# Broadcasting attention denominators through DRAM and transposing rows by DMA in a four-layer kernel on one core

## The chip, the core and the metric

The kernel runs on one core of a Trainium2 chip. The core has a matrix engine (TensorE; PE in the profile, its weight loads PEld), a vector engine (VectorE, DVE), an activation engine (ScalarE, ACT), GpSimd (POOL) and SyncE (SP), which here issues every DMA. Each engine takes its instructions in the order in which they were put on it and waits on semaphores. SBUF is the on-chip memory of 128 partitions; PSUM, in eight banks of 2 KB per partition, takes the results of matmuls.

The metric is the device time of one execution in microseconds, as a median of several runs.

## The reference

A sequence of 2048 rows of 576 numbers goes through four residual layers: linear attention (A), MLP (B), and once more A and B with the same weights.

```python
# A: x = x + attention(layernorm(x)); 32 heads of 18
qkv = layernorm(x) @ wqkv
phi = lambda t: jnp.where(t > 0, t + 1, jnp.exp(t)) + 1e-6
pq, pk = phi(q), phi(k)
kv  = einsum("bhsd,bhse->bhde", pk, v);  z = einsum("bhsd->bhd", pk)
o   = einsum("bhqd,bhde->bhqe", pq, kv) / (einsum("bhqd,bhd->bhq", pq, z) + 1e-6)
x   = x + o @ wo
# B: a second layernorm, then 576 -> 4608 -> 576
x   = x + gelu(layernorm(layernorm(x)) @ w1 + b1) @ w2 + b2
```

B's input is normalised twice in a row; the kernel folds the two into one by its constants. Matmul operands are bfloat16, sums are float32. Everything of A after the projections needs the sum `kv` over all 2048 rows, so an attention layer has two halves.

## The kernel before, in words

The 2048 rows are 16 row tiles of 128. The residual stream x lies in DRAM (`x_d`, float32) between layers. Every layer begins with the normalised rows transposed: `yT` holds 5 blocks of 128 columns (576 padded to 640) by 2048 rows, in bfloat16.

**Normalisation.** `LNPipe` holds row tiles on their way and `tick` (L232) moves each one stage on: load from `x_d` (L242, only in layers 1 and 3, for rows whose sum is long past), statistics on DVE (L249 to L260), the power -0.5 on POOL (L265), the normalised row `y` (L280 on POOL or L284 on DVE) into a ring of four buffers, and last five TensorE transposes into one PSUM bank of its own, `tp` (L297), with a copy to `yT` by ACT (L299) or DVE (L301). The loops of the layers call `tick` at fixed places.

**Attention, first half.** For each row tile: `k_proj` (L370), `v_proj` (L382, L385), and `kv_acc` (L400), which adds to the sums kv and z in PSUM. The feature map phi takes two ACT passes and two DVE passes (`phi_from_psum`). `q_proj` (L406) makes phi(q) for one of 5 head groups (7 heads of 18 are 126 partitions; the last group has 4) and one chunk of 512 rows; of its 20 calls 13 lie in the first half.

**Attention, second half, called the tail.** `kv_wo` (L451) multiplies kv by wo once per head group; `kvwo` is copied out by ACT (L458) or DVE (L456). `den_stage` (L466 to L476) makes the denominators of a chunk of 512 rows, their reciprocals on DVE, and spreads them with a mask into `quad_rden`. `scale_stage` (L482 to L485) broadcasts them over the 18 numbers of each head by a matmul with the 0/1 matrix `head_bc`, copies the result out of PSUM by ACT and multiplies phi(q) by it on DVE. `wo_stage` (L493) then makes the output rows of one row tile with ten matmuls in one of two two-bank PSUM buffers, and `residual` (L349) adds the old row, which `prefetch_xo` loaded four row tiles earlier into a ring of five buffers (`x_ring`; L333 in layer 0, as bfloat16 from the input, L336 later), into one of three `xn` buffers; L355 stores it. The first four row tiles of the next layer are normalised here.

**MLP.** Four chunks of 512 rows. Nine groups `m1_group` (L593) make the 4608 hidden numbers, gelu on ACT (L589); then for each of the chunk's four row tiles 72 matmuls (L640) make the output row. `feed_next` puts the next chunk's rows into `LNPipe`: two in the fifth and seventh group, two in the first output row. `tick(transposes=0)` keeps transposes out of the groups. In layer 1 every finished row also goes to `LNPipe` for layer 2.

**Order.** A planner puts the instructions of each engine into a list, from the order in which the program writes them and its own estimate of when each is ready; so an instruction written later can stand ahead (the load at L242 stands ahead of the last store of L355 at the end of each tail). Semaphore waits follow from that. `pe` chains the TensorE instructions of the layers in the written order, `chained` the early DMAs; `add_manual_dep` with `NOSYNC` only orders. The weights are loaded in pieces in layer 0's first half (`late_pieces`), w2 (L195) last, and POOL builds masks there (`masks`).

PSUM before: three banks for `h` (all projections, denominators, broadcasts, hidden numbers), one for `tp`, four for the two accumulators.

Of the kernel before, what the change touches and what calls it, by code (L numbers as in the profile page):

```python
# [15 lines left out]
P = 128  # L16
# [15 lines left out]
C1 = 1.0 + 1e-6  # L32


def build(tc, A_x, A_wqkv, A_wo, B_w1, B_b1, B_w2, B_b2, out, dbg=None, n_layers=4):
    nc = tc.nc
    dbg = dbg or {}
    with ExitStack() as ctx:
        const = ctx.enter_context(tc.tile_pool(name="const", bufs=1))
        ps_h = ctx.enter_context(tc.tile_pool(name="ps_h", bufs=3, space=PSUM))  # L40
        ps_tp = ctx.enter_context(tc.tile_pool(name="ps_tp", bufs=1, space=PSUM))
# [18 lines left out]
        head_bc = const.tile([P, G, P], BF16, name="head_bc")  # L60
        quad_mask = const.tile([P, 4, P], BF16, name="quad_mask")
# [12 lines left out]
        def inner_diag(tile_, lead, n):  # L74
# [5 lines left out]
        hb = head_bc[:, :, 0:126].rearrange("p g (h d) -> p g h d", h=7)  # L80
# [6 lines left out]
        ] + inner_diag(head_sel, lambda sign: [[126 * sign, G]], H) + [  # L87
            fill(quad_mask, 1.0),
            select(quad_mask[:], 0.0, ALU.is_ge, 0, [[-32, 4], [0, P]], 1),
            select(quad_mask[:], 0.0, ALU.is_ge, 31, [[32, 4], [0, P]], -1),  # L90
            fill(head_bc, 0.0),
        ] + [select(hb, 1.0, ALU.not_equal, -32 * quad, [[-7, G], [-1, 7], [0, DH]], 1) for quad in range(4)]
# [20 lines left out]
        NX = 5  # L113
        x_ring = [const.tile([P, D], F32, name=f"x_ring{i}") for i in range(NX)]
        x_d = dpool.tile([NT, P, D], F32, name="x_d")

        work = ctx.enter_context(tc.tile_pool(name="work", bufs=2))
        blk = ctx.enter_context(tc.tile_pool(name="blk", bufs=NF))

# [89 lines left out]
        def bias_casts():  # L209
# [4 lines left out]
                      [(lambda i=i: piece_w2(i)) for i in range(6)] + [piece_b1_dma]  # L214

        state = dict(ycnt=0, vcnt=0, xl=0)
        pool_last = dict(norm=None)
        dve_last = dict(norm=None, sum=None, phi=None)

        class LNPipe:  # L220
# [3 lines left out]
            def feed(self, xt, t, kind, norm_eng, evac_eng="dve", load_from=None, after=None):  # L224
                self.items.append(dict(stage=(0 if load_from is None else -1), xt=xt, t=t, kind=kind,
                                       norm=norm_eng, evac=evac_eng, load=load_from,
                                       after=after))

            def busy(self):
                return len(self.items)  # L230

            def tick(self, transposes=1):  # L232
                for it in list(self.items):
                    st = it["stage"]
                    if st == 4:
                        if transposes == 0:
                            continue
                        transposes -= 1
                    if st == -1:
                        xn = x_ring[3 + state["xl"] % 2]  # L240
                        state["xl"] += 1
                        load = nc.sync.dma_start(out=xn[:], in_=x_d[it["load"]])  # L242
                        if it["after"] is not None:
                            tc.add_manual_dep(load.ins, it["after"], NOSYNC, reason="loads give way")
                        it["xt"] = xn
                    elif st == 0:
                        xt = it["xt"]
                        stt = work.tile([P, 2, 6], F32, name="ln_st", bufs=4)
                        first = nc.vector.bn_stats(out=stt[:, 0, :], in_=xt[:, 0:HALF])  # L249
                        second = nc.vector.bn_stats(out=stt[:, 1, :], in_=xt[:, HALF:D])  # L250
                        if it["after"] is not None:
                            for stats in (first, second):
                                tc.add_manual_dep(stats.ins, it["after"], NOSYNC, reason="statistics give way")
                        mv = work.tile([P, 2], F32, name="ln_mv", bufs=6)
                        nc.vector.bn_aggr(out=mv[:], in_=stt[:])
                        u = work.tile([P, 1], F32, name="ln_u", bufs=4)
                        if it["kind"] == "A":
                            nc.vector.tensor_scalar(out=u[:], in0=mv[:, 1:2], scalar1=EPS, scalar2=None, op0=ALU.add)  # L258
                        else:
                            nc.vector.tensor_scalar(out=u[:], in0=mv[:, 1:2], scalar1=1.0 + EPS, scalar2=EPS * EPS,  # L260
                                                    op0=ALU.mult, op1=ALU.add)
                        it["mv"], it["u"] = mv, u
                    elif st == 1:
                        rstd = work.tile([P, 1], F32, name="ln_rstd", bufs=6)
                        nc.gpsimd.tensor_tensor(out=rstd[:], in0=it["u"][:], in1=neg_half[:], op=ALU.pow)  # L265
                        it["rstd"] = rstd
                    elif st == 2 and it["norm"] != "dve":
# [4 lines left out]
                    elif st in (2, 3):  # L272
# [14 lines left out]
                        if it["kind"] == "B":  # L287
                            nc.gpsimd.tensor_copy(out=y[:, D:DPAD], in_=y[:, 4 * P:D])
# [3 lines left out]
                    elif st == 4:  # L292
# [3 lines left out]
                        for k in range(KD):  # L296
                            pe(nc.tensor.transpose(out=tp[:, k, :], in_=y[:, k * P:(k + 1) * P], identity=ident[:]))  # L297
# [458 lines left out]
```

## Time and profile before

| | us |
|---|---|
| median of 3 runs | 790.49 (790.04 to 790.71) |
| profiled execution, its span | 790.0 |
| TensorE busy | 778.6 |
| ACT busy | 341.2 |
| DVE busy | 264.5 |
| POOL busy | 125.7 |
| layer 0: first half, and tail | 0 to 71, 71 to 112 |
| layer 1 (MLP) | 112 to 401 |
| layer 2: first half, and tail | 401 to 459, 459 to 501 |
| layer 3 (MLP) | 501 to 790 |

The profile is one execution. It shows the busy time of each engine, the span in 40 slices (a digit is the busy share in tenths; DMA is the mean share of 16 DMA engines), groups of instructions by line and tile, who waited for whom, the chain of work that ended last (followed back from the last instruction) and the time line of each engine. A time line gives start, duration, engine, line, operation, output and inputs, shapes and count. Matmuls are pipelined and their busy times overlap, so that the distance between starts tells what one costs. The DMA issues are listed with their size and the time from issue to landing.

### The profile page before, as it was taken

The page shows a single profiled execution, that of the slowest core. Times are in us where ns is not written, and L with a number is a line of the kernel's source. Part 1 is how long each engine was busy: PE and PEld are TensorE (multiplying, and loading weights), DVE is VectorE, ACT ScalarE, POOL GpSimd, SP SyncE. Part 2 cuts the span into 40 slices and gives each one's busy share as a digit, 9 for nine tenths or more (in the row PEclk, how much of TensorE's full clock was granted, in tenths as well). Part 3 has the DMA queues.
Part 4 walks back from the last instruction along what each step waited for, and adds up shares of the span by engine and source line. Part 5 has one row for each costly group of instructions (what it writes and reads, how often), then busy time and mean ns, then how long its engine had stood idle before and what let it go on. Part 6 is the DMA issues. An engine that isn't in the chain of part 4 may idle for free.

```text
span 790.0 us, 16121 instructions
## 1 busy us (share of the span) xinstructions
PE 778.6 (99%) x6807; PEld 507.0 (64%) x6813; DVE 264.5 (33%) x711; ACT 341.2 (43%) x754; POOL 125.7 (16%) x211
## 2 busy tenths in 40 slices
PE   8999999999999999999999999999999999999998
PEld 5776654685478458646887766547745864685476
DVE  6786862135023504300344478433200300010000
ACT  5888646304610660164047785471066017304600
POOL 4571402013010301200100004211110110001000
PEclk9999999999999999999999999999999999999999
DMA  9990372012021202200210007611210110011000
GB/s 274 259 285 24 129 260 71 1 62 90 1 61 46 76 2 75 76 1 1 80 42 1 2 16 240 240 47 53 61 39 3 60 61 1 9 46 38 2 23 23
DMA packets 43506, 56.92 MB, mean 72 GB/s; under 512 B 10283, under 2 KB 28075, under 8 KB 43435
## 3 DMA queue, kind: packets, MB, share of 16 engines
q1 hardware_dynamic: 43434, 55.91, 23.1%
q8 instruction: 53, 0.87, 0.5%
q14 instruction: 19, 0.15, 0.1%
HBM read 39.38 MB, written 16.52 MB: 71 GB/s over the span
## 4 chain that ended last, share of the span: by engine, by line
PE 92%; DVE 4%; DMA 2%; ACT 1%; issue 1%; POOL 0%; DVEq 0%; POOLq 0%; ACTq 0%
PE m_ps L640 36%; PE h_ps L593 20%; PE hp_ps L593 16%; PE q_ps L406 5%; PE k_ps L370 5%; PE v_ps L385 3%; PE tp L297 2%; PE v_ps L382 2%; PE wo_ps L493 2%; DMA x_d<-xn 2%; DVE xn L349 1%; PE kvacc L400 1%; PE warm_ps L171 1%; DVE pq L485 1%; DVE rden L474 0%
## 5 line engine op out<-in xcount | busy, mean ns | idle before, releaser
L640 PE MATMUL m_ps<-w_sb,hT 128*128 128x288 bf16 x2304 | 289.9, 286 | 0.0
L640 PEld LDWEIGHTS <-hT 128*128 128x128 bf16 x2304 | 223.2, 98 | 57.9 <-issue 3.4
L593 PEld LDWEIGHTS <-w_sb 64*128 64x128 bf16 x2304 | 124.5, 94 | 136.5 <-issue 1.9
L593 PE MATMUL hp_ps<-yT,w_sb 64*128 64x512 bf16 x1152 | 178.0, 376 | 0.0
L593 PE MATMUL h_ps<-yT,w_sb 64*128 64x512 bf16 x1152 | 148.0, 376 | 0.0
L598 ACT COPY relay_sb<-relay_sb 128x1 f32<-128x1 f32 x144 | 28.5, 198 | 276.3 <-PE h_ps L593 234.2
L589 ACT ACTIVATE hT<-h_ps,b1T 128x512 bf16<-128x512 f32 x144 | 91.0, 683 | 44.5 <-PE h_ps L593 44.5
L301 DVE COPY yT<-tp 128x640 bf16<-128x640 bf16 x40 | 19.6, 490 | 239.5 <-PE tp L297 239.5
L265 POOL TENSOR_TENSOR ln_rstd<-ln_u,neg_half 128x1 f32<-128x1 f32 x64 | 36.0, 562 | 357.5 <-DVE ln_u L258 193.5
L589 ACT ACTIVATE hT<-hp_ps,b1T 128x512 bf16<-128x512 f32 x144 | 91.1, 692 | 0.0
L339 POOL TENSOR_TENSOR x_ring<-x_ring,b_bc 128x576 f32<-128x576 f32 x32 | 40.8, 1279 | 159.5 <-DMA x_ring<-x_d 159.5
L593 PE MATMUL h_ps<-yT,w_tail 64*128 64x512 bf16 x144 | 54.1, 376 | 0.0
L593 PE MATMUL hp_ps<-yT,w_tail 64*128 64x512 bf16 x144 | 54.1, 376 | 0.0
L349 DVE TENSOR_TENSOR xbf<-m_ps,x_ring 128x576 bf16<-128x576 f32 x16 | 12.0, 752 | 117.6 <-PE m_ps L640 117.6
L406 PE MATMUL q_ps<-yT,wqkv_sb 128*126 128x512 bf16 (+1 forms) x200 | 50.0, 382 | 0.5 <-ACT phi_a L321 0.5
L493 PE MATMUL wo_ps<-kvwo,pq 126*128 126x288 bf16 (+1 forms) x320 | 43.8, 285 | 3.5 <-DVE xn L349 3.0
L370 PE MATMUL k_ps<-wqkv_sb,yT 128*128 128x288 bf16 x320 | 44.3, 286 | 0.0
L319 ACT ACTIVATE phi_e<-k_ps 128x288 bf16<-128x288 f32 x64 | 27.0, 422 | 35.9 <-PE k_ps L370 35.8
L493 PEld LDWEIGHTS <-pq 126*128 126x128 bf16 (+1 forms) x320 | 30.6, 97 | 14.8 <-issue 5.0
L322 DVE TENSOR_SCALAR phi_e<-phi_e 128x288 bf16<-128x288 bf16 (+2 forms) x104 | 30.7, 295 | 27.3 <-ACT phi_e L319 26.9
L593 PEld LDWEIGHTS <-w_tail 64*128 64x128 bf16 x288 | 27.1, 94 | 17.1
L370 PEld LDWEIGHTS <-yT 128*128 128x128 bf16 x320 | 30.9, 98 | 11.1
(90 smaller groups left out, 643.6 us busy)
## 6 DMA issues: line engine op xcount, KB each, us to landing
x_ring<-x_d SPq DMA_DIRECT2D x72, 288.0 KB, 3.0
x_d<-xn SPq DMA_DIRECT2D x48, 288.0 KB, 2.2
w_sb<-in_B_w_dram SPq DMA_DIRECT2D x6, 864.0 KB, 10.4
w_sb<-in_B_w_dram SPq DMA_DIRECT2D x9, 512.0 KB, 5.3
x<-in_A_x_dram SPq DMA_DIRECT2D x16, 144.0 KB, 4.1
x_ring<-in_A_x_dram SPq DMA_DIRECT2D x16, 144.0 KB, 3.2
out_dram<-xbf SPq DMA_DIRECT2D x16, 144.0 KB, 1.8
wqkv_sb<-in_A_wqkv_dram SPq DMA_DIRECT2D x3, 576.0 KB, 5.8
```

What stands on the lines that cost most here:

```text
L265: nc.gpsimd.tensor_tensor(out=rstd[:], in0=it["u"][:], in1=neg_half[:], op=ALU.pow)
L319: act_last["exp"] = nc.scalar.activation(out=e[0:rows, 0:n], in_=ps_ap, func=ACT.Exp).ins.name
L322: nc.vector.tensor_scalar(out=e[0:rows, 0:n], in0=e[0:rows, 0:n], scalar1=1.0, scalar2=1e-6, op0=ALU.min, op1=ALU.add)
L339: nc.gpsimd.tensor_tensor(out=xo, in0=xo, in1=b2_bc[:], op=ALU.add)
L370: pe(nc.tensor.matmul(kp[:, 0:HALF], lhsT=yT[:, k, tok], rhs=wqkv_sb[:, k, D + half * HALF: D + (half + 1) * HALF], start=(k == 0), stop=( ...
L385: pe(nc.tensor.matmul(vp[:, 1, 0:324], lhsT=yT[:, k, tok], rhs=wqkv_sb[:, k, 2 * D + 252: 3 * D], start=(k == 0), stop=(k == KD - 1)))
L406: pe(nc.tensor.matmul(qp[0:GR[g], :], lhsT=wqkv_sb[:, k, GO[g]:GO[g] + GR[g]], rhs=yT[:, k, c * CA:(c + 1) * CA], start=(k == 0), stop=(k ...
L493: pe(nc.tensor.matmul(wp[:, half, 0:HALF], lhsT=pq[(g, c)][0:GR[g], j * P:(j + 1) * P], rhs=kvwo[g][0:GR[g], half * HALF:(half + 1) * HALF ...
L589: act_last["gelu"] = nc.scalar.activation(out=hT[f][:, 0:CB], in_=dst[n], func=ACT.Gelu_apprx_tanh, bias=b1T[:, f:f + 1], scale=1.0).ins.name
L593: mm = pe(nc.tensor.matmul(dst[n], lhsT=wt, rhs=mv, start=(seen[n] == 0), stop=(seen[n] == 8)))
L598: relay = nc.scalar.copy(out=relay_sb[:, 1:2], in_=relay_sb[:, 0:1])
L640: pe(nc.tensor.matmul(acc[:, half, 0:HALF], lhsT=hT[f][:, j * P:(j + 1) * P], rhs=w2_sb[:, f, half * HALF:(half + 1) * HALF], start=(f == ...
```

## The change

It has these parts.

1. The reciprocal denominators `rden` of a chunk are stored to a DRAM tensor `rden_d` [32 heads, 2048 rows], and five loads per chunk bring them back, each head repeated over 18 partitions (`bcast_stage`). The broadcast matmuls, their copies on ACT, `quad_rden` and the masks `head_bc` and `quad_mask` go.
2. The rows of layers 1 to 3 (the second to fourth layer) are transposed by a DMA from `y` into `yT`, issued by SP. Layer 0's rows keep the TensorE transposes, whose PSUM tile now comes out of `h`, which has four banks instead of three.
3. One pool of nine row buffers takes the place of `x_ring` (5) and of `xn` (3). After layer 0 the sum is written over the row that was loaded.
4. For the four row tiles that are normalised in a tail, the sums for mean and variance come from two ACT passes with an accumulator; POOL makes the small numbers.
5. The order in the tail: all `q_proj` calls come ahead of the first `wo_stage`, with the first three `den_stage`; the broadcasts are issued up to a chunk or more ahead of their use. All `kvwo` copies are on ACT. The gelu table is loaded after the last phi.
6. The six pieces of w2 are loaded in the first six groups of layer 1 rather than in layer 0. `LNPipe` is rewritten with a generator per row (`row_steps`); in the groups of the MLP `tick` no longer holds transposes back.

```diff
+NROWS = 9
+AHEAD = 4
...
-        ps_h = ctx.enter_context(tc.tile_pool(name="ps_h", bufs=3, space=PSUM))
-        ps_tp = ctx.enter_context(tc.tile_pool(name="ps_tp", bufs=1, space=PSUM))
+        ps_h = ctx.enter_context(tc.tile_pool(name="ps_h", bufs=4, space=PSUM))
...
+        rden_d = dpool.tile([H, S], BF16, name="rden_d")
...
+        rows = ctx.enter_context(tc.tile_pool(name="rows", bufs=NROWS))
...
-                      [(lambda i=i: piece_w2(i)) for i in range(6)] + [piece_b1_dma]
+                      [piece_b1_dma]
+        w2_pieces = [(lambda i=i: piece_w2(i)) for i in range(6)]
...
+        def row_steps(xt, t, kind, norm_eng, evac_eng, stats, load_from, after):
...
+            if stats == "act":
+                y = y_ring[state["ycnt"] % NY]
+                state["ycnt"] += 1
+                nc.scalar.activation(out=y[:, 0:D], in_=xt[:, 0:D], func=ACT.Identity, accum_out=mv[:, 0:1])
+                nc.gpsimd.tensor_scalar(out=mv[:, 0:1], in0=mv[:, 0:1], scalar1=-1.0 / D, scalar2=None, op0=ALU.mult)
+                yield
+                nc.scalar.activation(out=y[:, 0:D], in_=xt[:, 0:D], func=ACT.Square, bias=mv[:, 0:1],
+                                     accum_out=mv[:, 1:2])
+                nc.gpsimd.tensor_scalar(out=u[:], in0=mv[:, 1:2], scalar1=(1.0 + EPS) / D, scalar2=EPS * EPS,
+                                        op0=ALU.mult, op1=ALU.add)
...
+            yield "transpose"
+            if evac_eng == "dma":
+                nc.sync.dma_start_transpose(out=yT[:, :, t * P:(t + 1) * P], in_=y[:])
+                return
+            tp = ps_h.tile([P, KD, P], BF16, name="tp", tag="h")
...
         def prefetch_xo(li, t, add_b2):
-            xo = x_ring[t % (3 if add_b2 else NX)]
+            row = row_tile("xo")
...
+            elif li == 0:
+                xn = row_tile("xn")
             else:
-                xn = work.tile([P, D], F32, name="xn", tag="xn", bufs=3)
+                xn = row
...
-                quad = blk.tile([P, D], BF16, name="quad_rden", tag="blk")
-                nc.vector.tensor_tensor(out=quad[:, 0:CA].rearrange("p (j n) -> p j n", j=4), in0=quad_mask[:],
-                                        in1=rden[:].unsqueeze(1).to_broadcast([P, 4, P]), op=ALU.mult)
-                quad_rden[c] = quad
+                nc.sync.dma_start(out=rden_d[:, c * CA:(c + 1) * CA].rearrange("h (j n) -> j h n", j=TPC),
+                                  in_=rden[:])
+
+            rden_bc = {}
+
+            def bcast_stage(c):
+                for g in range(G):
+                    heads = rden_d[7 * g:7 * g + GH[g], c * CA:(c + 1) * CA]
+                    rb = blk.tile([P, D], BF16, name="rden_bc", tag="blk")
+                    nc.sync.dma_start(out=rb[0:GR[g], 0:CA],
+                                      in_=heads.unsqueeze(1).to_broadcast([GH[g], DH, CA]))
+                    rden_bc[(g, c)] = rb
 
             def scale_stage(g, c):
-                bp = ps_h.tile([P, 512], F32, name="rden_ps", tag="h")
-                pe(nc.tensor.matmul(bp[:], lhsT=head_bc[:, g, :], rhs=quad_rden[c][:, 0:CA], start=True, stop=True))
-                rb = blk.tile([P, D], BF16, name="rden_bc", tag="blk")
-                act_last["copy"] = nc.scalar.copy(out=rb[0:GR[g], 0:CA], in_=bp[0:GR[g], :]).ins.name
                 nc.vector.tensor_tensor(out=pq[(g, c)][0:GR[g], 0:CA], in0=pq[(g, c)][0:GR[g], 0:CA],
-                                        in1=rb[0:GR[g], 0:CA], op=ALU.mult)
+                                        in1=rden_bc.pop((g, c))[0:GR[g], 0:CA], op=ALU.mult)
...
-                    lnp.feed(xn, t, "B", "pool", "act")
+                    lnp.feed(xn, t, "B", "pool", "dma", stats="act")
...
+            q_proj(*q_left.pop(0))
+            den_stage(0)
+            den_stage(1)
+            bcast_stage(0)
             kv_wo(0)
             q_proj(*q_left.pop(0))
+            kv_wo(1)
             q_proj(*q_left.pop(0))
+            kv_wo(2)
+            bcast_stage(1)
+            q_proj(*q_left.pop(0))
+            kv_wo(3)
+            q_proj(*q_left.pop(0))
+            kv_wo(4)
+            den_stage(2)
+            q_proj(*q_left.pop(0))
+            warm_table(ACT.Gelu_apprx_tanh, act_last["phi"])
+            for g in range(G):
                 scale_stage(g, 0)
...
                 wo_stage(t)
+                if t == 0:
+                    den_stage(3)
+                if j == 0 and c < 2:
+                    bcast_stage(c + 2)
                 if c + 1 < NCA:
                     for g in ((0, 1), (2, 3), (4,), ())[j]:
                         scale_stage(g, c + 1)
...
-                        lnp.feed(None, t, "B", "dve", "dve", load_from=t, after=(dve_last["sum"] if c == 0 else None))
+                        lnp.feed(None, t, "B", "dve", "dma", load_from=t, after=(dve_last["sum"] if c == 0 else None))
...
                         self.m1_group(c, g)
+                        if w2_pieces:
+                            w2_pieces.pop(0)()
...
-                        lnp.tick(transposes=0)
+                        lnp.tick()
...
-                            lnp.feed(xn, t, "A", "dve", "dve")
+                            lnp.feed(xn, t, "A", "dve", "dma")
```

## The prediction

> **What bounds the kernel now.** I read the page's busy shares first, then the costs of the pieces that the change takes off TensorE, then the two stretches in which TensorE is not full, then the DMA traffic in them.
>
> ```profile
> PE 778.6 (99%) x6807; PEld 507.0 (64%) x6813; DVE 264.5 (33%) x711; ACT 341.2 (43%) x754; POOL 125.7 (16%) x211
> ...
> DMA  9990372012021202200210007611210110011000
> ...
> PE m_ps L640 36%; PE h_ps L593 20%; PE hp_ps L593 16%; PE q_ps L406 5%; PE k_ps L370 5%; PE v_ps L385 3%; PE tp L297 2%; PE v_ps L382 2%; PE wo_ps L493 2%; DMA x_d<-xn 2%; DVE xn L349 1%; PE kvacc L400 1%; PE warm_ps L171 1%; DVE pq L485 1%; DVE rden L474 0%
> ```
>
> TensorE sets the time: 99% busy, 92% of the chain. DMA stands idle in most slices, but not in slices 25 and 26. A busy PE row overlaps its successor, so I price a matmul by the distance between starts. Layer 1's second product, and layer 0's attention tail, in the timeline of TensorE:
>
> ```profile
> 161.19 0.44 PE L297 MATMUL tp<-ident,y_ring 128*128 128x128 bf16 x5
> 161.47 3.10 PE L640 MATMUL m_ps<-w_sb,hT 128*128 128x288 bf16 x24
> ...
> 103.03 0.59 PE L482 MATMUL rden_ps<-quad_rden,head_bc 128*128 128x512 bf16 x2
> 103.47 1.40 PE L493 MATMUL wo_ps<-kvwo,pq 126*128 126x288 bf16 x10
> ```
>
> One row's five transposes hold TensorE 0.28 us (161.19 to 161.47), one denominator broadcast 0.22 (two from 103.03 to 103.47). The busy times of the two tails, of layer 2 and of layer 0 (columns: stretch, length, busy PE, PEld, DVE, ACT, POOL, clock, DMA share, GB/s), then short stretches at the end of layer 2's:
>
> ```profile
> 459.00:501.18 42.18, 39.16 (x351) 25.91 (x354) 33.97 (x83) 25.23 (x46) 9.63 (x16) 1.00 0.53 174
> 70.70:112.14 41.44, 39.02 (x351) 25.92 (x354) 34.04 (x83) 25.23 (x46) 9.69 (x16) 1.00 0.43 140
> ...
> 484.00:488.00 4.00, 3.74 (x52) 2.41 (x51) 2.46 (x6) 2.28 (x4) 2.90 (x6) 1.00 0.86 282
> ...
> 494.00:496.00 2.00, 2.00 (x18) 1.58 (x17) 1.18 (x2) 1.49 (x2) 0.00 (x0) 1.00 1.03 389
> 496.00:498.00 2.00, 1.08 (x9) 0.71 (x8) 0.53 (x1) 0.00 (x0) 0.00 (x0) 1.00 1.03 366
> ```
>
> In the tails TensorE idles and at 494 to 498 the DMA engines are full: 389 and 366 GB/s are what they give at most. The chain in order of time says who waits there, and the DMA issues of 470 to 505 what is moved:
>
> ```profile
> 485.32 3.75 DMA x_d<-xn
> ...
> 493.98 4.81 DMA x_d<-xn
> ...
> x_d<-xn SPq DMA_DIRECT2D x16, 288.0 KB, 3.0
> x_ring<-x_d SPq DMA_DIRECT2D x15, 288.0 KB, 3.9
> ```
>
> The residual sum waits for a store to free one of three xn buffers.
>
> **Transposes outside the tails.** The 48 rows of layers 1 to 3 leave TensorE. Eight of them lie in the tails (below). The other 40 lie in stretches where TensorE never waits (72 to 73 us busy of 72 to 73 per MLP chunk, 56 of 56 in layer 2's first half): 40 x 0.28 = 11.2 us gained in full, if no yT row comes late. In a chunk the rows are loaded from the fifth group on and needed one product later, some 30 us; DMA is 0.16 busy there. Their 40 DVE copies (0.49 us each) go too and are worth nothing, DVE being a third busy.
>
> What one DMA transpose costs is not in the trace. Each of 128 partitions gets five runs of 256 bytes, 640 runs per row. Below: an output store of 144 KB lands in 1.8 us. Above: the w_tail load, 32 KB in 128 such runs, lands in 4.8 us, so five of them one after another 24. Those w_tail loads leave the queue 0.60 to 0.65 us apart, so five are 3.2; I take 3.2 us per row of queue and engines and 5 to land, by that row, nearest in its short runs. SP carries 48 more issues; in MLP chunks it mostly waits for DVE (285 us for L349), so that is covered.
>
> [...]
>
> **The tails: work that goes.** From the last kvacc (459.27) to the MLP's first matmul (501.12) pass 41.9 us; in layer 0 41.1 (70.96 to 112.08). TensorE's own work in it, by distances of starts: 7 q_ps x 1.08, z_ps 0.35, 5 kvwo x 0.26, 4 den_ps x 0.56, 20 rden_ps x 0.22, 4 tp x 0.28, 16 wo_ps x 1.23 = 36.7 us; so 5.2 and 4.4 us are waits. After the change rden_ps (4.4) and tp (1.1) are gone: 31.2 us. I split it at the first wo_ps: before it 10.9 (all 7 q_ps, z, 5 kvwo, 3 den), after it 20.3 (16 wo and the fourth den).
>
> **The tails: the new wait ahead of the first wo_ps.** From the end of the first den_ps run: reciprocal finished 1.3 us later (462.72 to 464.06), a store of 3.0 (the tail's x_d row), four more issues of 0.43, a load of 3.9 (the tail's row), a scale of 0.42: 10.3 us. TensorE has 8.3 meanwhile (two den, 5 kvwo, 5 q_ps, 0.5 of wo_ps ahead of the last head group). The wait is 2.0. Ends: 0 with a store of 1.8 and a load of 3.0, 5.4 with 4.8 and the slowest load of the tail, 5.5. I take the tail's own medians. The other three chunks have their broadcast issued a chunk (4.9 us) or more ahead of the scales. SP is held while it waits for the store; behind it are only residual rows needed later.
>
> **The tails: DMA after the first wo_ps.** Layer 2 must move, in that stretch, 12 rows of loads (3.54 MB; four came ahead), 12 stores (3.54; the last four may land later), two chunks of broadcast (each 576 rows of 1 KB, 1.18) and four transposes (0.66): 8.9 MB. At the mean of the three full stretches, 358 GB/s (320 at 492 to 494, 389, 366), 24.9 us, more than TensorE's 20.3. Bounds: 22.9 at 389, 31.6 at 282. Layer 2's tail is 10.9 + 2.0 + 24.9 = 37.8, a gain of 4.1. In layer 0 the loads are half as large: 7.1 MB, 19.8 us, under TensorE's work (25.2 at 282).
>
> [...]
>
> **The tails: statistics of the first four rows** go from DVE (two 0.37, 0.13, 0.1 by starts: 3.9 us per tail) to ACT (8 passes like a 576-wide kvwo copy, 0.65: 5.2 us, where 20 rden_bc copies of 0.53 went) and POOL (8 more of 0.54, 4.3 on top of 9.6: 13.9). POOL is now late: the first sum ends 2.1 us after the first wo_ps, POOL needs 13.9, hand-overs some 1.4, the last transpose 5: the MLP can begin at 22.4. In layer 0 that exceeds 20.3; in layer 2 the DMA covers it. Layer 0: 10.9 + 2.0 + 22.4 = 35.3, a gain of 5.8. If a transpose lands in 1.8, TensorE's 20.3 rules.
>
> **Edits at nothing.** Nine shared row buffers end the wait for xn (2.1 us at most, in waits), already counted by rebuilding the tail; in layer 0 four rows held by POOL and five loaded fill the nine, so sum 5 may wait about a microsecond, inside the 22.4. Two kvwo copies per layer go to ACT (0.65 each; before the first wo_ps ACT has 10.3 us of work in 12.9). The eight mask steps on POOL and eight quad multiplies on DVE were off the chain. The six w_sb loads of 864 KB move into layer 1's first product: 5.3 MB at 285 GB/s is 19 us, inside its 35; without that cover the second product would wait for the rest. The four-bank pool takes layer 0's transposes in with the projections: 0, at most 1 us either way (no wait named tp as releaser but ACT's and DVE's own).
>
> **Sum.** 11.2 + 4.1 + 5.8 = 21.1 us. The profiled execution has a span of 790.0, the median run is 790.5, so 0.5 lies around it: 790.0 - 21.1 + 0.5 = 769.4.
>
> **Rivals.** Fast: both tails find no wait and DMA runs at 389: 33.8 and 31.2 us, 29 gained, 761. For it, the loads spread to nine buffers; against it, the 282 at 484 to 488.
>
> Slow transposes, slower than before: the rows go through one queue, so the tail cannot end before the first y (about 8 us after the first wo_ps) and four transposes. With T per row the tails grow by 8 + 4T beyond 24.9 and 22.4, together 8T - 31.3, which eats 21.1 at T = 6.6 us. At 8 us the time is 802; from 9 us layer 1's chunks (8 rows in 72.7 us) are bound too. For it, the bound of 24 and the w_tail rows; against it, 160 KB is little beside 288 KB stores that land in 2.2.
>
> DMA-bound tails: at 282 GB/s with the 5.4 us wait they take 47.9 and 41.5, the one 6.0 slower, the other 0.4: 786. For it, the full DMA at 494; against it, TensorE was also busy there.
>
> **How the numbers follow.** Forecast 0.52 (764 to 778), fast 0.12 (758 to 764), DMA-bound tails 0.14 (778 to 789), T near its break-even 0.02, slow transposes 0.20. Within 0.2%, 1.6 us, about what a measurement of this kernel can tell from no change, counts as same. Faster 0.78, same 0.02, slower 0.20. The range 758 to 790 leaves out the slow transposes.
>
> **What would show it.** Right: TensorE has no gap between m_ps groups, the tails take 35 and 38 us, the first wo_ps waits for a DVE scale behind a DMA, and layer 2's DMA share is 0.9 after it. Wrong: a DMA transpose of over 6 us, h_ps waiting for yT, or DVE's sums waiting for row loads held on SP behind a transpose.

## The result, and the profile after

The changed kernel takes 802.18 us (median; 800.66 to 803.78) against 790.6 for the kernel before on the same chip: 1.0145 times as long, with a 95% interval from 1.0128 to 1.0162. The forecast was 769.4. The profiled execution has a span of 801.3 us, 11.3 more than before. Of the page of the changed kernel, the busy times, the granted TensorE clock in 40 slices (in tenths of full speed), and the chain:

```profile
PE 768.1 (96%) x6533; PEld 495.5 (62%) x6533; DVE 235.9 (29%) x627; ACT 329.4 (41%) x742; POOL 119.6 (15%) x219
...
PEclk9999779999999999999999998899999999999999
...
PE m_ps L646 35%; PE h_ps L597 19%; PE hp_ps L597 16%; PE q_ps L409 5%; PE k_ps L373 5%; DMA rden_bc<-rden_d 4%; PE v_ps L388 3%; PE v_ps L385 2%; PE wo_ps L495 2%; PE kvacc L403 1%; SPq L482 1%; DMA xo<-x_d 1%; PE tp L282 1%; SPq L278 1%; DVE pq L487 0%
```

TensorE is busy 10.5 us less and no longer full: 96% of the span, where it was 99%. Two things are new: broadcast loads are 4% of the chain, and the clock digits fall to 7 and 8 in the two tails, where before all forty were 9.

I measure a tail from the start of the last kvacc group to the first h_ps. Layer 0's was 41.4 us and is 54.5, layer 2's was 42.1 and is 51.7: 13.2 and 9.6 longer, 22.7 together before rounding. The rest of the kernel is therefore 11.4 us shorter. The gain outside is there; the tails lost twice as much.

The timeline of TensorE in layer 0's tail (start, duration; in brackets the idle time and what ended it), some lines of it:

```profile
78.74 0.41 PE L454 MATMUL kvwo_ps<-wo_sb,kvT 126*126 126x288 bf16 x2 [1.70 <-ACT kvwo L458]
...
83.40 0.53 PE L495 MATMUL wo_ps<-kvwo,pq 126*128 126x288 bf16 x3
...
89.69 0.30 PE L464 MATMUL den_ps<-pq,zsel 126*32 126x128 bf16 x4 [3.63 <-DVE pq L325]
...
91.34 6.71 PE L495 MATMUL wo_ps<-kvwo,pq 126*128 126x288 bf16 x30
99.62 2.62 PE L495 MATMUL wo_ps<-kvwo,pq 126*128 126x288 bf16 x20 [1.58 <-DVE xn L352]
...
108.71 2.56 PE L495 MATMUL wo_ps<-kvwo,pq 126*128 126x288 bf16 x10 [4.70 <-DVE xn L352]
111.97 12.79 PE L495 MATMUL wo_ps<-kvwo,pq 126*128 126x288 bf16 x80 [0.71 <-DVE xn L352]
```

The first wo_ps starts at 83.40, and 41.3 us pass from it to the MLP at 124.70 (38.5 in layer 2). Ahead of it TensorE waits for a kvwo copy of ACT. Its waits after it are for DVE: for phi in front of the fourth den_ps, for sums that free an accumulator later. The last line holds 80 matmuls (eight row tiles) that take 12.79 us with no wait among them; at the 1.23 per row tile of before they would take 9.84. What DVE itself waits for is in the waits (us in total, times, longest) and in the chain in order of time (start, us, what):

```profile
DVE pq L487 <- DMA rden_bc<-rden_d: 22.4, 25, 2.8
...
DVE xo L352 <- DMA xo<-x_d: 9.9, 7, 2.6
...
PE wo_ps L495 <- DVE xn L352: 7.4, 4, 4.7
...
PE kvwo_ps L454 <- ACT kvwo L458: 3.4, 2, 1.7
```

```profile
82.90 4.94 DMA rden_bc<-rden_d
...
95.90 5.55 DMA rden_bc<-rden_d
...
101.82 0.76 DVE xn L352
...
104.56 5.92 DMA rden_bc<-rden_d
```

The load of chunk 1 for which DVE waits last lands at 87.84, that of chunk 2 at 101.46, that of chunk 3 at 110.47. TensorE needs 4.9 us per chunk; these landings are 13.6 and 9.0 apart. Each of them takes 5 to 6 us, and on SP loads of chunks 2 and 3 (L482) stand behind stores that wait for DVE: of denominators (L473, at 89.39 and 92.93) and of rows (L358, at 92.42 and 102.60). The clock and the DMA engines of after, by stretches (columns: stretch, length, busy PE, PEld, DVE, ACT, POOL, clock, DMA share, GB/s):

```profile
88.00:94.00 6.00, 3.41 (x24) 2.01 (x24) 4.46 (x11) 1.64 (x4) 0.53 (x3) 0.50 0.24 73
...
112.00:118.00 6.00, 6.00 (x27) 3.83 (x27) 2.10 (x3) 0.00 (x0) 0.00 (x0) 0.53 1.03 317
...
500.00:506.00 6.00, 3.32 (x19) 2.15 (x19) 1.98 (x4) 0.00 (x0) 0.00 (x0) 0.78 1.01 261
```

At 88 to 94 the DMA engines are a quarter busy while chunk 2's denominators are on their way out and its first load back: it is delay, not amount. At 112 and 500 they are full, at less than the 389 GB/s of before.

### The profile page after: what moved, and what is told of

It reads as the page before. It is cut to its first block, busy times and chain, and to the rows that moved or that the text cites. A ratio compares the mean times of both kernels' runs of the same rounds, so it can differ in the third digit from the quotient of the medians.

```text
span 801.3 us, 15624 instructions
## 1 busy us (share of the span) xinstructions
PE 768.1 (96%) x6533; PEld 495.5 (62%) x6533; DVE 235.9 (29%) x627; ACT 329.4 (41%) x742; POOL 119.6 (15%) x219
## 4 chain that ended last, share of the span: by engine, by line
PE 89%; DMA 4%; DVE 2%; SPq 2%; issue 1%; ACT 1%; POOL 0%; DVEq 0%; POOLq 0%; ACTq 0%
PE m_ps L646 35%; PE h_ps L597 19%; PE hp_ps L597 16%; PE q_ps L409 5%; PE k_ps L373 5%; DMA rden_bc<-rden_d 4%; PE v_ps L388 3%; PE v_ps L385 2%; PE wo_ps L495 2%; PE kvacc L403 1%; SPq L482 1%; DMA xo<-x_d 1%; PE tp L282 1%; SPq L278 1%; DVE pq L487 0%
## 5 line engine op out<-in xcount | busy, mean ns | idle before, releaser
L646 PE MATMUL m_ps<-w_sb,hT 128*128 128x288 bf16 x2304 | 283.6, 286 | 0.0
L352 DVE TENSOR_TENSOR xbf<-m_ps,xo 128x576 bf16<-128x576 f32 x16 | 12.1, 758 | 226.3 <-PE m_ps L646 226.3
L340 POOL TENSOR_TENSOR xo<-xo,b_bc 128x576 f32<-128x576 f32 x32 | 40.8, 1278 | 239.4 <-DMA xo<-x_d 184.3
L495 PE MATMUL wo_ps<-kvwo,pq 126*128 126x288 bf16 (+1 forms) x320 | 54.7, 338 | 15.0 <-DVE xn L352 7.4
L352 DVE TENSOR_TENSOR xo<-m_ps,xo 128x576 f32<-128x576 f32 x16 | 12.1, 758 | 169.3 <-PE m_ps L646 169.3
L495 PEld LDWEIGHTS <-pq 126*128 126x128 bf16 (+1 forms) x320 | 36.3, 114 | 33.0 <-issue 16.0
```

What stands on the lines that cost most here:

```text
L340: nc.gpsimd.tensor_tensor(out=xo, in0=xo, in1=b2_bc[:], op=ALU.add)
L352: total = nc.vector.tensor_tensor(out=xn[:].rearrange("p (h n) -> p h n", h=2), in0=halves, in1=xo.rearrange("p (h n) -> p h n", h=2), op= ...
L495: pe(nc.tensor.matmul(wp[:, half, 0:HALF], lhsT=pq[(g, c)][0:GR[g], j * P:(j + 1) * P], rhs=kvwo[g][0:GR[g], half * HALF:(half + 1) * HALF ...
L646: pe(nc.tensor.matmul(acc[:, half, 0:HALF], lhsT=hT[f][:, j * P:(j + 1) * P], rhs=w2_sb[:, f, half * HALF:(half + 1) * HALF], start=(f == ...
```

## The experiments

First theory (A): the gain outside the tails is real, and the broadcast by DMA loses it in the tails. Rivals: the transposes lose it (B), or the new order on DVE (A1, against A2, the broadcast being late by itself), or the falling clock (C1). The runs that take the change apart, with medians in us; the others (e4, e7, e8, e12 to e16) are below. All of the table have the "outer transposes", the 40 rows outside the tails by DMA. The tails are those of the one profiled execution, which for e6 was its longest (781.3). The kernel before took 790.6 to 790.9 beside all runs.

| run | broadcast | tail rows | order | first-row statistics, kvwo copies | us | tails |
|---|---|---|---|---|---|---|
| after | DMA | DMA | new | ACT | 802.2 | 54.5, 51.7 |
| e3, old tail and buffers | matmul | TensorE | old | DVE, shared | 779.8 | 41.2, 40.6 |
| e6, old tail in the kernel after | matmul | TensorE | old | DVE, shared | 779.8 | 44.2, 40.4 |
| e11 | DMA | TensorE | old | DVE, shared | 812.9 | 55.8, 58.5 |
| e10 | matmul | TensorE | old | ACT | 785.1 | 44.0, 44.1 |
| e9 | matmul | TensorE | new | DVE, shared | 789.3 | 47.1, 45.2 |
| e17, as e9, late table | matmul | TensorE | new | DVE, shared | 783.6 | 43.6, 42.7 |
| e5 | matmul | TensorE | new | ACT | 789.1 | 45.6, 46.1 |
| e1 | matmul | DMA | new | ACT | 787.8 | 44.9, 45.7 |
| e2 | DMA | TensorE | new | ACT | 796.2 | 49.4, 48.0 |

### Outer transposes alone (e3)

```diff
 # kernel before
-lnp.feed(None, t, "B", "dve", "dve", load_from=t
+lnp.feed(None, t, "B", "dve", "dma", load_from=t
-lnp.feed(xn, t, "A", "dve", "dve")
+lnp.feed(xn, t, "A", "dve", "dma")
+if it["evac"] == "dma":
+    nc.sync.dma_start_transpose(out=yT[:, :, t * P:(t + 1) * P], in_=y[:])
```

> The kernel before with one part of the change alone: the 40 rows of layers 1 to 3 that are normalised outside the tails are transposed by a DMA from SP, everything else as before. The prediction's term: 40 rows x 0.28 us, so 11.2 us less, 779.3 us; the tails stay at 41.1 and 41.9 us. If a DMA transpose delays a yT block or the row loads behind it on SP, 782 us or more.

Measured: 779.80 us, 0.9859 of before (0.9844 to 0.9874), so 11 us gained and the tails as short as before. The transposes' row (ns min/median/max of one issue) and the list of DMA issues (count, median us to landing), both of e3:

```profile
L296 SPq DMA_TRANSPOSE yT<-y_ring x40: 1199/1201/2040, 118.7 to 532.7; - x40
```

```profile
yT<-y_ring SPq DMA_TRANSPOSE x40, 3.1
```

A whole 128x640 row costs SP 1.2 us and lands in 3.1, as fast as the 288 KB row loads of the same run (also 3.1). This version is faster than both kernels.

### The matmul broadcast put back (e1), and the tail rows on TensorE (e2, e5)

```diff
 # e1
-rden_d / bcast_stage: one store, five loads per chunk
+quad_rden[c] = quad_mask * rden;  head_bc matmul into rden_ps
+nc.scalar.copy(out=rb[0:GR[g], 0:CA], in_=bp[0:GR[g], :])
 # e2
-lnp.feed(xn, t, "B", "pool", "dma", stats="act")
+lnp.feed(xn, t, "B", "pool", "act", stats="act")
 # e5: both
```

> The changed kernel with one part undone: the denominators are broadcast by the matmul with head_bc and copied by ACT, as before (the mask quad_mask is kept narrow so that nine row buffers still fit); order, DMA transposes, row pool and statistics on ACT stay. Theory A (the round trip through DRAM and the DVE scales that wait for it cost the tails 13.1 and 9.4 us): the tails fall from 54.2 and 51.3 us to 38 to 41 each, TensorE's work in them being 35.6 us, the clock stays at 1.0, and the time is 772 to 778 us. Theory B (the first four rows' DMA transposes hold SP and fill the DMA engines, so row loads come late): the layer 2 tail stays above 46 us and the time at 788 or more.

> The changed kernel with the four row tiles of each tail transposed on TensorE again and copied by ACT (8 of the 48 rows); the other 40 stay with the DMA. Theory A: the waits for the broadcast stay, TensorE gets 1.1 us per tail back to do, so 798 to 804 us. Theory B: SP loads the residual rows 5 to 8 us earlier in layer 2, the sums' waits for them (9.9 us in all) go, and the time falls to 790 to 795 us.

> The changed kernel with both parts of the tail undone: denominators broadcast by matmul and the four row tiles of each tail transposed on TensorE; the new order, the row pool, the statistics on ACT and the other 40 DMA transposes stay. If the two costs add (14.3 us for the broadcast and 6.0 us for the four transposes, by the two runs that undid one each), 802.2 - 20.3 = 782 us. If the transposes hurt only because they share SP and the DMA engines with the broadcasts, 786 to 788 us. What lies above 779.8 us then belongs to the order of the tail and to the work moved to ACT.

Measured: e1 787.84 (0.9961 of before; 0.9946 to 0.9975), e2 796.16 (1.0071; 1.0055 to 1.0088), e5 789.12 (0.998; 0.9971 to 0.999). Taking the broadcast off DMA gives back 14.3 us, the larger part; A holds, but e1 did not come down to its 772 to 778. Taking the eight tail rows off DMA gives back 6.0 while the broadcasts are on DMA, so e2 ended between the ranges of A and B. When the broadcasts are not on DMA it costs 1.3 (789.1 against 787.8), which the intervals hardly tell from nothing; e5 ended above both of its ranges. So the transposes cost only beside the broadcasts. Layer 2 shows where: on SP of after the loads of old rows stand behind the transposes, and the sums wait for them. Whether the queue makes them late or the engines, which are full then, is not shown. SP in after, then the waits of e2, where the 9.9 us of after are 2.0:

```profile
497.34 1.25 SPq L278 DMA_TRANSPOSE yT<-y_ring  x1
498.70 0.51 SPq L337 DMA_DIRECT2D xo<-x_d  x1
```

```profile
DVE xo L352 <- DMA xo<-x_d: 2.0, 2, 1.3
```

With neither on DMA, e5 is still 9.3 us above 779.8.

### What the order and the work on ACT cost (e6, e9, e10, e17)

```diff
 # e6: e5, and kv_wo / q_proj / den_stage / scale_stage in the order of before,
 #     statistics on DVE, odd kvwo copies on DVE, gelu table at row 13
 # e9: e6 with the new order and its early table
 # e10: e6 with statistics and all kvwo copies on ACT
 # e17: e9, and
-warm_table(ACT.Gelu_apprx_tanh, act_last["phi"])
+if t == NT - 3:
+    warm_table(ACT.Gelu_apprx_tanh, act_last["copy"])
```

> The changed kernel with the tail as before: its order, matmul broadcasts, kvwo copies on ACT and DVE in turn, statistics of the four row tiles on DVE and their transposes on TensorE. What stays of the change: 40 DMA transposes, nine shared row buffers with sums in place, four banks, w2 loaded in layer 1. If the shared rows end the waits of the sums for stores (5.2 us in all before) and for POOL (4.1 us), 773 to 778 us. If those waits were not what held TensorE, 779 to 781 us, as with the 40 transposes alone.

> The kernel after, with its order in the tail and its early gelu table, but broadcasts by matmul, first-row statistics and every other kvwo copy on DVE, and the eight tail rows transposed on TensorE. Against the version with the whole old tail (779.8 us) it differs by the order and the place of the table load alone. If the order carries what the matmul broadcast did not give back (789.1 us with that order and with the work on ACT), the time is 786 to 789, and the first wo_ps stands behind the scales of chunk 0 that wait for ACT. If the work on ACT carries it, the time is 779 to 782.

> The old tail (779.8 us) with the statistics of the first four rows on ACT and POOL and all kvwo copies on ACT, as the kernel after has them; order, matmul broadcasts and table load are the old ones. If the work on ACT carries the 9 us that are left between 789.1 and 779.8, the time is 785 to 789. If the order carries it, 779 to 782. If both are needed, so that the copies of the broadcasts wait behind the work only in the new order, both this and the version with the new order alone come out at 779 to 783.

> The new order alone (789.3 us) with the gelu table loaded three rows before the end of the tail, as in the kernel before. If the load ahead of chunk 0's copies is what the order costs, each tail loses 1.3 us and, with the slow clock that follows the wait, up to 4: 781 to 787. If the order itself costs (five broadcasts in a row ahead of the first wo_ps, each waiting for ACT's copy and DVE's scale), 787 to 790.

Measured: e6 779.82 (0.9862; 0.9844 to 0.988), the same as e3: nine shared buffers, the four-bank pool and the late w2 loads together are worth nothing that can be measured. e9 789.26 (0.9983; 0.9973 to 0.9992), e10 785.05 (0.9929; 0.9914 to 0.9944), e17 783.61 (0.9907; 0.9891 to 0.9924). The order costs 9.4, the work on ACT 5.2, both together (e5) 9.3, so the two don't add. Of the order's 9.4, one instruction carries 5.7: the load of the gelu table, 1.28 us on ACT ahead of chunk 0's copies. ACT in e9, and one stretch of e9, then of e17:

```profile
83.40 1.28 ACT L322 ACT_TABLE_LOAD   x1
...
84.80 2.50 ACT L498 CAST rden_bc<-rden_ps 126x512 bf16<-126x512 f32 x5
```

```profile
88.00:94.00 6.00, 6.00 (x48) 3.37 (x47) 4.40 (x10) 1.55 (x3) 0.00 (x0) 0.61 0.22 76
```

```profile
88.00:94.00 6.00, 5.11 (x37) 3.47 (x36) 6.00 (x17) 2.73 (x5) 1.95 (x4) 1.00 0.46 148
```

Without the load the clock stays at 1.00, and the tails are 3.5 and 2.5 us shorter, where 1.28 was taken out. In e9 TensorE waits 1.61 us for the last copy, and behind that wait the clock is 0.50 from 85.89 to 92.72, with TensorE busy for 6.6 of these 6.8 us: the wait is paid again in a slower clock.

In after the same table load stands in a gap of ACT. Layer 2:

```profile
479.61 1.28 ACT L314 ACT_TABLE_LOAD   x1
...
484.17 0.68 ACT L231 ACTIVATE y_ring<-xo 128x576 bf16<-128x576 f32 x1 [3.07 <-issue]
```

There are no copies of broadcasts that could stand behind it. So the early table is a cost of e1, e5 and e9 that after does not have, and the DMA broadcast may cost more than the 14.3 and 7.0 that the differences to e1 and e5 give, by up to some 5.7. No run has the work on ACT, matmul broadcasts and the late table together.

### The DMA broadcast in the old order (e11)

```diff
 # e6, and
-quad_rden[c] = quad;  rden_ps matmul and copy
+nc.sync.dma_start(out=rden_d[...], in_=rden[:])
 den_stage(c)
+bcast_stage(c)
```

> The old tail (779.8 us) with one thing of the change in it: the denominators are broadcast by DMA, each chunk's five loads issued right behind its den_stage, in the old order. If the broadcast is late by itself, the time is above 795: 10 us from the first den_ps to the first loads landing, 8.5 us of SP for two chunks, and the old order has only two q_ps and a kvwo_ps between. If the new order's early den_stage was what hurt, the time is 780 to 786, with rden_ps (4.4 us per tail) gone from TensorE.

Measured: 812.90 us, 1.0281 of before (1.0244 to 1.0319): the broadcast by DMA alone costs 33.1 us against 779.8. TensorE, and then DVE, in e11:

```profile
87.09 2.56 PE L498 MATMUL wo_ps<-kvwo,pq 126*128 126x288 bf16 x10 [5.35 <-DVE kvwo L459]
```

```profile
81.08 0.42 DVE L490 TENSOR_TENSOR pq<-pq,rden_bc 126x512 bf16<-126x512 bf16 x1 [1.18 <-DMA rden_bc<-rden_d]
...
85.61 0.42 DVE L490 TENSOR_TENSOR pq<-pq,rden_bc 72x512 bf16<-72x512 bf16 x1 [0.37 <-DMA rden_bc<-rden_d]
...
86.29 0.75 DVE L459 CAST kvwo<-kvwo_ps 126x576 bf16<-126x576 f32 x1
```

The scales wait on DVE, and phi and a kvwo copy that TensorE needs stand behind them. The loads of chunks 2 and 3 also leave later than in after, at 100.0 and 112.1 us in layer 0 and not at 91.6 and 101.2. So the new order and the work on ACT are a cover that the DMA broadcast needs: with them it costs 7.0 us (e2 against e5), without them 33.1. Which of them covers is not shown. For the matmul broadcast they are a loss.

### What in the broadcast is slow (e8, e12)

```diff
 # e8: loads of 256 columns, used twice
-out=rb[0:GR[g], 0:CA], in_=heads...to_broadcast([GH[g], DH, CA])
+out=rb[0:GR[g], 0:CA // 2], in_=heads[:, 0:CA // 2]...to_broadcast([GH[g], DH, CA // 2])
 # e12
-nc.sync.dma_start(out=rb[0:GR[g], 0:CA],
+(nc.gpsimd if g % 2 else nc.sync).dma_start(out=rb[0:GR[g], 0:CA],
```

> The changed kernel with each broadcast load half as wide: 256 of the 512 columns of a chunk are loaded and used for both halves, so half of the rows are scaled by a wrong denominator; 126 pieces of 512 bytes in place of 1 KB, as many loads as before. Theory D1 (bytes on some six or seven engines set the pace of the loads, 0.85 us each): SP's issues come 0.45 us apart, DVE's waits for the broadcasts (22.4 us) fall by half, 793 to 797 us. Theory D2 (the issue of 126 pieces on SP sets the pace): 0.7 us apart as before, 799 to 803 us.

> The kernel after with the loads of head groups 1 and 3 issued by POOL's queue and not SP's: two of the five broadcasts of each chunk go beside the other three, with the same pieces and bytes. If the one queue of SP limits (0.73 us per issue, 3.7 per chunk), a chunk takes 2.2 us of SP and the ten loads of chunks 0 and 1, which leave SP over 8.5 us, leave in some 5.1: each tail is 3 us or more shorter and the time 794 to 797. [...] POOL's own issues could also be slower than SP's: then chunk 2 and 3, whose loads stand behind POOL's small steps, come later, and the time is above 804.

Measured: e8 795.61 (1.0063; 1.0039 to 1.0087), 6.6 less than after; e12 800.45 (1.0113; 1.0095 to 1.013), which the intervals don't tell from after. Half the bytes in as many pieces, first e8's issues and waits, then e12's issues from POOL and what that queue (q0) moved in all (packets, MB, share of 16 engines):

```profile
L482 SPq DMA_DIRECT2D rden_bc<-rden_d x40: 638/732/917, 77.5 to 487.9; - x40
```

```profile
DVE pq L489 <- DMA rden_bc<-rden_d: 14.2, 17, 2.9
```

```profile
L482 POOL DMA_DIRECT2D rden_bc<-rden_d x16: 598/608/846, 77.9 to 496.9; - x16
```

```profile
q0 software_dynamic: 1536, 2.08, 0.9%
```

An issue takes 0.73 us whether a piece is 1 KB or 512 bytes, and not the 0.45 of D1; what fell in e8 is DVE's wait, from 22.4 to 14.2, and the time came into D1's range. In e12 the first ten loads left in 4.9 us instead of 8.5, and it gained nothing that the intervals show: SP's issuing alone isn't the limit. Its pieces were not the same ones, contrary to what was expected: POOL's queue moved most of its bytes of chunks 0 and 1 in packets of 4 KB, 209 ns each.

In after's packets the first ten loads are 1152 pieces of 1 KB, mean 48 ns, and from 82 to 88 us 5.9 of 16 engines are busy. From their first packet to the end of their last pass 9.5 us in after, 8.5 in e8 and 8.0 in e12, so neither fewer bytes nor faster issues alone makes chunks 0 and 1 much shorter. In layer 0 chunk 2's packets take 7.9 us in after, 5.9 in e8, 6.1 in e12, and chunk 3's 7.1, 4.8 and 5.4. As e12 shortens them almost as much and does not gain, the landing of these loads alone doesn't explain e8's 6.6 us; what else half the bytes changed is not shown.

### Order on DVE, and the clock (e4, e7)

```diff
 # e4
+tc.add_manual_dep(mul.ins, dve_last["phi"] if c == 0 else dve_last["sum"], NOSYNC)
 # e7, ahead of den_stage(3)
+for _ in range(14):
+    pe(nc.tensor.matmul(fill_ps[:], lhsT=wqkv_sb[:, 0, 0:P], rhs=wqkv_sb[:, 0, 0:512], ...))
```

> The changed kernel with the order on DVE alone altered: scales of the first chunk stand behind the last phi, those of later chunks behind the sum of the row tile at which they are written. Theory A1 (DVE's order: scales that wait for broadcasts stand ahead of the last phi(q), so the fourth den_ps waits 8.2 us in all and the clock falls): that wait goes, the clock stays higher, 790 to 796 us. Theory A2 (the broadcast itself is late, about 0.8 us per load on few engines after a 3 us landing): the wait moves to wo_ps behind the scales and the time stays at 798 to 803 us.

> The changed kernel with 14 extra matmuls of 512 columns (3.0 us at full clock) in each tail between the first wo_ps and the fourth den_ps, where TensorE waits 4.5 and 3.6 us for DVE; their result is not used. Theory C1 (the clock, granted at 0.50 and 0.58 after that wait, costs by itself, about 3 us per tail): the clock stays near 1.0 there and the time falls to 795 to 798 us. Theory C2 (the slow matmuls only fill time in which the broadcasts and row loads are awaited anyway): 800 to 804 us.

Measured: e4 801.11 (1.0127; 1.0111 to 1.0143), no difference from after that the intervals show, so that order alone isn't the cause. e7 807.38 (1.0208; 1.0192 to 1.0223), 5.2 longer than after and outside the ranges of both theories. Two of its stretches, and the wo_ps between them:

```profile
88.00:94.00 6.00, 4.23 (x48) 2.60 (x47) 2.93 (x7) 1.65 (x4) 1.02 (x4) 1.00 0.28 89
...
100.00:106.00 6.00, 6.00 (x32) 3.93 (x31) 1.94 (x3) 3.81 (x10) 4.00 (x11) 0.61 0.80 274
```

```profile
98.58 8.03 PE L495 MATMUL wo_ps<-kvwo,pq 126*128 126x288 bf16 x40 [5.29 <-DVE xn L352]
```

The fill kept the clock at 1.00 from 88 to 94 (0.50 in after), and TensorE only came earlier to the next wait; behind that, the clock fell to 0.61 in the mean of 100 to 106. The 6.0 us of added matmuls cost 5.2. So e7 moved the slow clock and did not take it away: what the clock costs by itself it doesn't tell. Each slow stretch in after's tails begins in a wait (at 86.97, 107.45, 482.92 and 503.40 us, in waits of 3.63, 4.70, 0.96 and 2.68), so the slow clock came with waits here; but it is not free. The 80 matmuls from 111.97 to the MLP, without a wait, were 3.0 us slower than at full clock (12.79 against 9.84).

### The round between SP and DVE (e13 to e16)

The chain suggested a second theory: loads of a chunk stand on SP behind stores that wait for sums, which stand on DVE behind scales that wait for the loads of the chunk before.

```diff
 # e13; e14 with e4's edit too; e15 = e13 with e2's; e16 = all three
-nc.sync.dma_start(out=x_d[t], in_=xn[:])
+(nc.sync if li % 2 else nc.scalar).dma_start(out=x_d[t], in_=xn[:])
```

> The kernel after with the stores of residual rows in the two attention layers issued by ACT's queue and not SP's, nothing else. In layer 0 the loads of chunk 3 leave SP at 101.15 and from 102.98 us, behind a store that waits for a sum; without that store they can leave behind chunk 2's last load (96.5), some 5 us earlier, and in layer 2 the same (from 494.2 back to 489.1). If this round between SP and DVE is the cause, each tail is 4 to 5 us shorter and the time 791 to 795. If the landing of the loads is the cause, 799 to 803.

> The one before, and on DVE the scales stand behind the last phi and the sums, so that the reciprocals of chunks 2 and 3 no longer wait behind scales. If both legs of the round count, this is 2 to 4 us faster than with the stores alone (788 to 792): chunk 2's store of denominators would leave at some 84 us and not at 89.4. If the landing of the loads is the cause, it is at 799 to 803 like the order alone (801.1).

> Stores of residual rows in the attention layers on ACT's queue, and the eight tail rows transposed on TensorE. With the rows on TensorE alone the time was 796.2. If the round between SP and DVE costs, and its gain was lost in engines filled by the transposes, it shows here: 789 to 793. If the round is not on the path, 795 to 798. In both cases broadcasts still come by DMA, so the 789.1 of the same kernel with broadcasts by matmul is the lower end.

> The one before with DVE's scales behind the last phi and the sums as well. If both legs of the round count and the transposes hid it, 787 to 791; if neither counts, 794 to 798.

Measured: e13 801.02 (1.0132; 1.0099 to 1.0166), e14 801.17 (1.0138; 1.011 to 1.0167), e15 802.42 (1.0142; 1.0109 to 1.0176), e16 795.19 (1.005; 1.0033 to 1.0067). None is faster than the run with which it compares (after for e13 and e14, e2 for e15 and e16) by more than the intervals, and e15 lies above both of its ranges. The theory fell as a price: in e13 chunk 3's loads leave at 98.3 to 102.6 instead of 101.2 to 106.0, in e14 DVE waits for broadcasts 0.8 us and no longer 22.4 (1.8 in e4, by the order alone), and the time stays. New waits took their place. One of e14's, both times in layer 0:

```profile
DVE xn L352 <- POOL y_ring L267: 7.9, 2, 6.0
```

The sum waits for a row buffer until POOL has normalised the second row (in e16 for 5.1 us); ACT's second pass for that row stands behind a store that e13 put on ACT, issued at 98.52 in e14. These runs thus moved a cost to ACT as they took it off SP, and don't tell what the round alone costs.

## Why the prediction was wrong

**Transposes outside the tails: right.** 40 x 0.28 = 11.2 us were forecast; e3 gained 11, and after's part outside the tails is 11.4 shorter. No yT row came late.

**The price of a DMA transpose: within its bounds, taken too high.** Taken as 3.2 us of queue and engines and 5 to land; measured 1.2 on SP and 3.1 to land (e3). On the engines it is more than its bytes: a row by itself is 640 packets of 256 bytes at 21 ns, 13.5 engine-us, 0.84 us of all 16 engines, and the 28 rows of e3 in layer 1 are 1.16 in the mean, where I had counted 0.16 MB at 358 GB/s, 0.46. The slow-transposes rival, which gave 802 at 8 us per row, ends at the measured time by luck: its mechanism is false. Per engine a row by itself gives 12 GB/s (256 bytes in 21 ns), against 24 in the full stretch of before (389 over 16).

**Ahead of the first wo_ps: the number right, partly by luck.** 12.9 us were forecast with a wait of 2.0 for the first broadcast; measured 13.2 from the last kvacc group's start (70.16 to 83.40). But the wait there is 1.70 for a kvwo copy of ACT, which had been put at nothing; the scales of chunk 0 hold the first wo_ps only by 0.6, after its start.

**After the first wo_ps: the step that failed.** 22.4 and 24.9 us were forecast, 41.3 and 38.5 measured, 32.5 too little together, which is the miss of 32.8 but for 0.3. Two things in it were wrong.

The first is the sentence that the other three chunks have their broadcast issued a chunk or more ahead of the scales. They are written so; but chunk 2's first load left at 91.55 and its last landed at 101.46, and chunk 3's landed at 110.47. I priced the broadcasts as bytes in a shared stream, 1.18 MB of 8.9, and not as a chain of store, issue, landing and scale per chunk. What stood on SP behind a waiting store was not only residual rows needed later, but broadcast loads too; and in layer 2 the row loads that stood behind transposes came late (9.9 us of DVE's waits), the last of the prediction's own signs of being wrong.

The second is a term at nothing: every matmul was priced at the full clock of before. In layer 0 the 41.3 us are the 20.3 of work that were forecast, 12.5 of waits and 8.5 more; 30 matmuls took 6.71 for 3.69, ten 2.56 for 1.23 and 80 12.79 for 9.84, which is 7.3 of these. In layer 2 there are 10.7 of waits and 7.5 more. Waits of 2.1 and 4.6 had been forecast, so of the 32.5 some 16.5 are waits and 16.0 slower matmuls. This splits the time line and is no price, since without the slow clock TensorE would have come earlier to its next wait (e7).

By parts the runs show, from e6 to after: the order with its early table and the work on ACT 9.3 (e5), the broadcast by DMA in that order 7.0 (e2), the tail rows by DMA beside it 6.0; none had been forecast as a loss. Other ways through the parts give other shares: 14.3 for the broadcast where the tail rows go by DMA, 33.1 in the old order; and 5.7 of the order's 9.4 in e9 are the table load, which stands in a gap of ACT in after, so that the DMA broadcast's share is rather too small.

**The engines of a broadcast load: fewer than taken.** The rate that I had put on the broadcasts' bytes, 358 GB/s, is that of stretches in which the engines were 0.91 to 1.03 busy. From 82 to 88 us of after, with loads of chunks 0 and 1 under way, 5.9 of 16 engines were busy, at 126 GB/s.

**POOL as the second bound: not reached.** Its eight small steps were priced at 0.54 us each and take about 0.2; in layer 0 POOL is done at 106.7 and the MLP begins at 124.7. The wait for a row buffer in layer 0, put at about a microsecond, became visible (5.1 to 6.0) only in e14 and e16.

**Edits at nothing: partly right.** Row buffers, PSUM pool and late w2 together are worth nothing (e6). The kvwo copies on ACT were put at nothing; with the statistics there they cost 5.2 (e10), and 1.7 per tail of TensorE's waits in after are for one of them. The gelu table's earlier place, which I didn't price, costs 5.7 us beside matmul broadcasts.

**DMA-bound tails: seen in part.** The engines are full only at the end of each tail (share 1.0 at 112 and 500), where layer 2's sums wait for row loads. The rival gave 786 for full engines through the whole of it.

Open stays how the 14.3 us divide between the landing of the loads and the round through SP and DVE: e8 (6.6 for half the bytes) changes more than the landing, and e13 to e16 don't isolate the round.

## What to carry to other kernels

Price a transfer between two engines' steps as a chain (store, issue, landing, use) for each round, and follow on the queue's real order what stands ahead of it; a spare DMA bandwidth of three quarters says nothing about that. Split a change that has several parts: here the part with 40 transposes was worth 11 us alone, and it was lost behind a broadcast worth -33 in one order and -7 in another. A microsecond put on an engine ahead of TensorE's next operand cost 2.0 and 2.7 here (1.28 us of table load, 2.5 and 3.5 per tail).

## What the hardware showed unexpectedly

The granted clock fell in or just behind waits of TensorE, to 0.50 for 7 to 10 us at a time in after and e9. In after it was 0.50 from 86.97 to 97.21 us, with a wait of 3.6 us that ended at 89.69, and 30 matmuls of wo_ps took 6.71 us where 3.7 are usual; it was 0.50 again from 107.45 to 117.69, with a wait of 4.7. In e9 a wait of 1.61 us behind a 1.28 us table load was enough (0.50 from 85.89 to 92.72), and 1.00 came back without the load (e17); but the wait of 1.70 us at 78.74 in after left the clock at 1.00.

The loads that repeat 7 heads over 126 partitions (the fifth of a chunk 4 over 72) kept 5.9 of 16 engines busy in after from 82 to 88 us, at 48 ns per piece of 1 KB from SP's queue; POOL's queue moved most of its loads' bytes in packets of 4 KB at 209 ns (e12, chunks 0 and 1).

A DMA transpose of one row is 640 packets of 256 bytes, 21 ns each where it ran by itself, and 37, 51 and 37 in the mean in three rows of after (issued at 401.20, 525.00 and 597.51 us) beside each of which only one 16 KB packet of the instruction queue ran. In the tails of after these packets took 0.41 of the engines' time in layer 2 at 500 to 506 us, where the share of all was 1.01 at 261 GB/s, and 0.61 in layer 0 at 106 to 112, where it was 1.00 at 166.
